# Gated linear attention into an MLP mixer: batch 2 of the channel mixer's input transposed by TensorE in place of the DMA crossbar, with a new order of all instructions

## Chip, cores and metric

One core of one Trainium2 chip. The metric is device time in microseconds; lower is better. Kernel before: 169.14 us, median of 3 runs (169.07 to 169.2).

Short names: PE is TensorE (matmuls; its weight loads are PEld), DVE VectorE, ACT ScalarE, POOL GpSimd, SP SyncE. SP and ACT issue all DMAs, on a queue each.

## What is computed

From q, k, v and alpha, all of shape (4 batches, 8 heads, 768 steps, 48), a recurrence over time, and then a token and channel mixer on its result:

```python
for t in range(S):
    state = alpha[:, :, t, :, None] * state + einsum('bhd,bhe->bhde', k[:, :, t], v[:, :, t])
    y[:, :, t] = einsum('bhd,bhde->bhe', q[:, :, t], state)
x = y.transpose(0, 2, 1, 3).reshape(B, S, H * D)          # (4, 768, 384)
h = maximum(x.transpose(0, 2, 1) @ w_tok1, 0) @ w_tok2     # 768 -> 256 -> 768
u = x + h.transpose(0, 2, 1)
out = u + maximum(u @ w_ch1, 0) @ w_ch2                    # 384 -> 1536 -> 384
```

Inputs, weights and output are float32 in HBM; the matmuls take bf16.

## The kernel before

**Attention** is cut into 12 pieces n = 0 to 11, three of 256 steps for each of the four batches. A piece loads alpha, k, q and v (ld_at, ld_kt, ld_qt, ld_vt; 384 KB each), takes logarithms (ln, for pieces from 3 on P, ln1, lnP, r1), sums them by matmul (cum, cumw for pieces 0 to 2), takes exponentials (E, IE, Et), scales q and k with them (q0r, k0a, qq, kk), casts v to bf16 (vb, and vs0, vs1 for swapped halves), and transposes scaled q and k: pieces 0 to 5 on PE (trq, trk) with a copy out (evq, evk), pieces 6 to 11 by DMA (dq, dk, pq). Then come two half blocks of 128 steps: scores (G0, G1), their mask on DVE (mask0, mask1), key-value sums (K), states (s, sa, sm), outputs (ia, ib for the state's part, y0, y1 for the block's own), and x0, x1, which copy the result to bf16. A number behind the name is the piece: y1_2 is the second half block of piece 2.

**The mixer** runs batch by batch. t1_b_m_i multiplies the six x of a batch with w_tok1, ht is its relu, t2_b_i multiplies with w_tok2, and u_b_i adds x. For the channel mixer u has to be transposed. For batches in `UP` (lines 101 and 300 to 308) PE does it: up_b_p, three groups of six 128x128 transposes into PSUM (`utr`, line 798, matmul at line 803), and ut_b_p, three copies to SBUF on DVE or ACT (`utev`, line 805). For the others SP issues two DMA transposes, ux_b_0 and ux_b_1, one for three u each (`uxbar`, line 667). c1_b_mc_half is the product with w_ch1 (three matmuls of 384 columns, line 811): 12 blocks mc by two halves of the steps; with `UP` a c1 of half 0 waits for ut_0 and ut_1 and one of half 1 for all three, without it for its own ux. rt is its relu on DVE or ACT, c2_b_i_q the product with w_ch2 (line 816), four parts for each of six row blocks i, o adds u, and st stores 192 KB.

**Weights** are loaded in pieces of 384 KB into the same 19 buffers as q, k, v and alpha (`in`) and cast to bf16 by POOL, ACT or DVE: cw_wt10, wt11 (w_tok1), wt20, wt21 (w_tok2), wc10 to wc15 (w_ch1; the first three for mc 0 to 5, the others for mc 6 to 11), wc20 to wc25 (w_ch2; c2's part q needs the pieces that hold its three mc). A load into a used buffer waits until the last reader of the earlier content is done, and its queue waits with it.

**The order** is written out. `ORDER` (line 363) names every operation once, in program order, with a letter for the engine (t PE, s ACT, v DVE, g POOL, y SP); each engine works through its own in that order. `BUFS` (line 432) gives the buffer of every value. Both are the outcome of a search with a planner's costs (lines 35 to 62); the search itself is not in the kernel. [...] And f1_ and f3_ operations are fills: one or three matmuls of 512 columns on zeros (`fill`, line 595), put ahead of PE's operations of pieces 0 to 2 into a PSUM bank that is free; they compute nothing that is used.

```python
UP = (0, 1)                                        # line 101
...
        if b in UP:                                # line 300
            for p in range(3):
                bank = V("one")
...
        else:
            for half in range(2):
                uts.append(P.op(f"ux_{b}_{half}", {"SP": (1240.0, 1240.0)}, ...
```

Of the kernel before, what the change touches and what calls it, by code (L numbers as in the profile page):

```python
# [100 lines left out]
UP = (0, 1)  # L101
# [14 lines left out]
def build(g):  # L116
# [154 lines left out]
    def mixer(b):  # L271
# [27 lines left out]
        uts = []  # L299
        if b in UP:  # L300
            for p in range(3):
# [62 lines left out]
ld_at1s ld_at0y ld_kt0s ld_qt0y ld_qt1s ld_vt0y f1_cumw1t f1_cumw0t f3_cumw0t f3_cumw1t ld_kt1y f3_G00t ln0s ln1s  # L364
cumw0t ld_at2y cumw1t E0s f1_trq0t IE0s qq0v f1_G00t Et0s ld_vt1y IE1s kk0v f1_trk1t trq0t E1s f1_trk0t trk0t Et1s
vb0s f1_trq1t f1_K0t ld_vt3y evk0v qq1g evq0s K0t f3_trk1t s0_0v ld_qt2y ld_at3s sa1_0v vs0_0g vs1_0s f1_G10t kk1v
ld_kt3y ld_kt2s G1_0t G0_0t ln2s trq1t mask0_0v vb1g trk1t evq1s f3_K1t ldw_wt10y sm1_0g mask1_0v K1t evk1s f1_cumw2t
cumw2t sa0_1v vb3g f3_y1t sm0_1v E2s f1_G01t vs0_1g sa1_1v ia1t G0_1t ln13s P3v f1_trq2t Et2s ld_vt2y IE2s f1_y1t
mask0_1v sm1_1g ld_at4y lnP3s f1_y0t vs1_1v cum3t qq2v y0_0t E3s f3_trq2t r13s x0_0v ib0t ldw_wt20y IE3s y1_0t trq2t
k0a3v ld_qt3y x1_0s ib1t kk2v ldw_wt11y y0_1t f3_G11t kk3v cw_wt10s vs1_3s x0_1s f1_G11t G1_1t f1_K2t evq2s mask1_1v  # L370
f1_trk2t vb2g trk2t vs0_3g K2t ldw_wt21y evk2v y1_1t ldw_wc14y trk3t vs1_2g sa0_2v x1_1s ldw_wc13y kb3s f1_G12t
t1_0_1_0t P4v ldw_wc12y t1_0_1_1t G1_2t ka3v lnP4s sm0_2v f1_G02t ia2t kc3s mask1_2v G0_2t vs0_2g evk3s f3_y2t
cw_wt20g q0r3g f1_y2t mask0_2v ld_at5s t1_0_0_0t t1_0_0_1t ldw_wc15s ib2t t1_0_1_2t cw_wt11s cum4t y1_2t y0_2t qq3g
K3t x1_2v x0_2s t1_0_0_2t t1_0_1_3t s0_3v ld_kt4s t1_0_0_3t t1_0_1_4t cw_wt21s t1_0_1_5t t1_0_0_4t sa1_3v t1_0_0_5t
cw_wc14g ht_0_1s ht_0_0v trq3t E4s t2_0_0t ldw_wc11s t2_0_3t cw_wc13g IE4s u_0_0v t2_0_1t evq3s u_0_3v t2_0_5t ld_qt4y
t2_0_2t u_0_1v t2_0_4t ldw_wc10y u_0_2v up_0_0t cw_wc12s ld_qt5y u_0_5v G0_3t ld_kt5y G1_3t P5g ut_0_0s u_0_4v up_0_1t
up_0_2t ut_0_1v lnP5s cw_wc15g ib3t mask0_3v ut_0_2s cum5t c1_0_9_0t ln14s c1_0_11_1t mask1_3v ldw_wc20s c1_0_8_1t
rt_0_11_1s sm1_3g k0a4g c1_0_8_0t r14s rt_0_9_0v ldw_wc21y c1_0_7_0t rt_0_8_1s rt_0_8_0v cw_wc11s c1_0_10_1t y0_3t
y1_3t rt_0_7_0v kk4v c1_0_6_1t ld_at6s IE5s c1_0_9_1t E5s rt_0_6_1v cw_wc10g ld_vt4y rt_0_10_1s c1_0_11_0t rt_0_9_1v
ldw_wc22y x1_3v trk4t q0r4v c1_0_2_1t c1_0_1_0t evk4s rt_0_11_0v qq4g c1_0_3_0t x0_3s c1_0_4_0t rt_0_1_0s ld_vt6y  # L380
rt_0_3_0v ln15s c1_0_3_1t ldw_wc23y k0a5v ldw_wc24s rt_0_2_1s c1_0_4_1t c1_0_0_0t r15s kk5v cw_wc20s trq4t rt_0_3_1s
rt_0_0_0v cw_wc21g evq4s ka4g q0r5g c1_0_5_1t c1_0_5_0t rt_0_4_1v c1_0_0_1t trk5t rt_0_5_0s ldw_wc25y ld_vt5y
rt_0_5_1v rt_0_4_0v c1_0_10_0t qq5g ld_at7s c1_0_7_1t rt_0_0_1v vb4s G0_4t rt_0_7_1v c1_0_2_0t mask0_4v c1_0_6_0t
cw_wc22g ld_kt6y rt_0_2_0s c1_0_1_1t ln16s evk5v ld_at9y c2_0_0_0t vs0_4s vb6g kb4s ia4t rt_0_10_0v y0_4t kc4s trq5t
x0_4v rt_0_6_0s c2_0_1_0t c2_0_1_1t c2_0_2_0t P6v rt_0_1_1s evq5v vs1_4s cw_wc23g vs0_6s K4t ld_kt7s cw_wc24g
c2_0_4_0t lnP6s sa0_4v c2_0_4_1t cw_wc25s ld_qt6y sm0_4v c2_0_2_1t ld_qt8y r16s sa1_4v c2_0_1_2t vs1_6s cum6t sm1_4g
ld_qt7s G1_4t E6s mask1_4v c2_0_2_2t vb5s c2_0_4_2t IE6s vs1_5g c2_0_2_3t t1_1_1_0t kc5s P7g c2_0_1_3t vs0_5s o_0_2v
ld_at8s c2_0_4_3t o_0_1v k0a6g ln17s K5t t1_1_1_1t lnP7s c2_0_0_1t sa0_5v ld_at10s c2_0_0_2t kk6g o_0_4v r17s G0_5t
st_0_1s G1_5t mask0_5v c2_0_5_0t c2_0_5_1t ib4t P9g dk6y mask1_5v y1_4t t1_1_1_2t ia5t x1_4s t1_1_0_0t y0_5t st_0_4y
c2_0_5_2t x0_5s sm0_5v lnP9s t1_1_1_3t q0r6v t1_1_0_1t t1_1_1_4t ib5t ld_vt7s q0r7v y1_5t t1_1_0_2t c2_0_0_3t qq6v  # L390
x1_5s ln18s t1_1_0_3t cum7t k0a7v t1_1_1_5t t1_1_0_4t IE7s t1_1_0_5t c2_0_5_3t ht_1_1s ht_1_0v dq6y ka6s c2_0_3_0t P8v
E7s t2_1_0t t2_1_2t o_0_0v r18s kb6g kk7g u_1_0v u_1_2v t2_1_3t st_0_2s ld_qt9y c2_0_3_1t t2_1_1t t2_1_4t ld_vt8s
u_1_3v ld_kt8s t2_1_5t kc6s u_1_1v ln110s c2_0_3_2t up_1_1t q0r8g u_1_5v st_0_0y dk7y u_1_4v up_1_0t ut_1_0s K6t cum9t
vb7g ut_1_1v o_0_5v IE9s vs0_7v P10g c2_0_3_3t E9s s0_6v up_1_2t ln19s pq6s ut_1_2v c1_1_6_0t c1_1_9_0t kb7g qq7g
c1_1_10_1t o_0_3v sa1_6v ld_at11s c1_1_8_1t rt_1_10_1v r19s c1_1_6_1t rt_1_6_0v ld_kt11s c1_1_7_0t lnP8s rt_1_8_1v
sm1_6g dq7y c1_1_10_0t ka7s rt_1_6_1v c1_1_11_0t c1_1_5_1t rt_1_10_0s vs1_7v rt_1_7_0v rt_1_9_0s r110s cum8t rt_1_5_1v
c1_1_4_0t IE8s vb8v c1_1_1_1t rt_1_4_0s ld_kt9s rt_1_11_0v c1_1_9_1t c1_1_0_0t q0r9v rt_1_1_1s c1_1_3_1t c1_1_2_0t
vs1_8v E8s rt_1_0_0s qq8v rt_1_9_1s c1_1_5_0t c1_1_8_0t kc7s rt_1_3_1s dq8y P11g rt_1_2_0v rt_1_8_0s K7t ld_kt10s
c1_1_11_1t c1_1_7_1t rt_1_5_0s sa0_7v ld_vt9y c1_1_4_1t ld_qt10s sm0_7v rt_1_7_1s sa1_7v k0a8g c1_1_2_1t rt_1_11_1s
st_0_3y rt_1_4_1v c1_1_0_1t rt_1_2_1s c1_1_1_0t sm1_7v rt_1_0_1s kk8v G0_6t rt_1_1_0s G1_6t lnP11s c2_1_4_0t ib6t  # L400
mask1_6v vs0_8s dk8y lnP10s c2_1_3_0t mask0_6v k0a9g pq7g st_0_5y c1_1_3_0t c2_1_3_1t c2_1_4_1t c2_1_3_2t rt_1_3_0s
pq8s qq9v y0_6t y1_6t x0_6s kk9v c2_1_3_3t c2_1_4_2t x1_6s G0_7t o_1_3v G1_7t dk9y vb9v cum10t mask1_7v t1_2_0_0t
c2_1_4_3t E10s kb9g c2_1_0_0t ln111s vs0_9s ka9g dq9y o_1_4v c2_1_0_1t IE10s vs1_9g mask0_7v k0a10g st_1_4s ld_vt10y
c2_1_0_2t kc8s ib7t c2_1_1_0t q0r10v kc9s G1_8t r111s mask1_8v kk10g c2_1_0_3t c2_1_1_1t t1_2_0_1t o_1_0v y1_7t K8t
x1_7s G0_8t sa0_8v dk10y st_1_3s c2_1_1_2t mask0_8v sm0_8g c2_1_1_3t ia7t y0_7t qq10g pq9s o_1_1v ia8t t1_2_1_0t
cum11t x0_7v K9t y0_8t t1_2_1_1t s0_9v E11s ib8t y1_8t t1_2_1_2t IE11s t1_2_0_2t k0a11g sa1_9v t1_2_0_3t dq10y x0_8s
t1_2_1_3t x1_8v G0_9t G1_9t mask0_9v t1_2_1_4t ld_vt11y t1_2_1_5t t1_2_0_4t t1_2_0_5t ht_2_1s st_1_1y c2_1_2_0t ka10g
ht_2_0s mask1_9v kk11g c2_1_2_1t kb10s t2_2_3t vb10s t2_2_5t u_2_3v t2_2_4t ib9t u_2_5v y1_9t kc10g sm1_9g t2_2_1t
u_2_4v x1_9s pq10g t2_2_0t c2_1_2_2t ux_2_1y u_2_0v y0_9t u_2_1v t2_2_2t vs0_10g x0_9s c2_1_2_3t G0_10t c2_1_5_0t
ia10t vs1_10s ld_qt11s mask0_10v c2_1_5_1t c2_1_5_2t u_2_2v K10t o_1_2v y0_10t ux_2_0y c2_1_5_3t sa0_10v x0_10s  # L410
c1_2_4_1t o_1_5v sm0_10g c1_2_11_1t st_1_5y dk11y rt_2_4_1s c1_2_8_1t rt_2_11_1s q0r11g sa1_10v c1_2_9_1t st_1_2y
c1_2_2_1t rt_2_9_1v qq11g c1_2_5_1t rt_2_2_1v c1_2_0_1t c1_2_7_1t rt_2_0_1v rt_2_5_1v c1_2_4_0t vb11g rt_2_7_1s dq11y
c1_2_0_0t c1_2_1_0t sm1_10v rt_2_0_0s c1_2_1_1t vs0_11v rt_2_8_1v st_1_0y kc11s rt_2_4_0s rt_2_1_1v c1_2_10_0t
c1_2_10_1t rt_2_1_0v c1_2_3_1t rt_2_10_1v pq11g c1_2_3_0t rt_2_3_1v c1_2_7_0t rt_2_3_0v K11t c1_2_6_1t rt_2_10_0v
sa0_11v c1_2_9_0t rt_2_6_1s c1_2_2_0t sm0_11g rt_2_9_0v vs1_11s rt_2_7_0s G1_11t G1_10t mask1_11v G0_11t c2_2_4_0t
c2_2_4_1t mask0_11v c2_2_4_2t c2_2_4_3t ib11t y1_11t mask1_10v x1_11s c1_2_5_0t ib10t t1_3_1_0t t1_3_1_1t t1_3_0_0t
rt_2_5_0v o_2_4v t1_3_0_1t y1_10t st_2_4y x1_10v ia11t t1_3_0_2t y0_11t t1_3_1_2t c1_2_11_0t x0_11v rt_2_2_0v
t1_3_1_3t t1_3_0_3t t1_3_1_4t t1_3_1_5t c2_2_5_0t c1_2_8_0t rt_2_8_0s ht_3_1s rt_2_11_0s c1_2_6_0t t1_3_0_4t t1_3_0_5t
c2_2_5_1t c2_2_0_0t rt_2_6_0s c2_2_5_2t ht_3_0s c2_2_5_3t t2_3_4t o_2_5v t2_3_1t t2_3_3t u_3_4v st_2_5y c2_2_1_0t
t2_3_5t t2_3_0t u_3_3v c2_2_0_1t u_3_5v c2_2_0_2t c2_2_0_3t o_2_0v u_3_0v u_3_1v c2_2_1_1t t2_3_2t u_3_2v ux_3_1y  # L420
c2_2_3_0t ux_3_0y c2_2_3_1t c2_2_2_0t c2_2_3_2t st_2_0y c2_2_2_1t c2_2_1_2t c2_2_2_2t c1_3_3_1t c2_2_2_3t c1_3_8_1t
# [453 lines left out]
```

## Time and profile before

| what | value |
|---|---|
| median of the runs | 169.14 us (169.07 to 169.2) |
| the profiled execution: time, span | 169.17 us, 167.4 us |
| mean granted clock of PE | 0.990 |
| PE busy | 159.3 us, 1752 matmuls |
| of it fills (line 593, zs) | 15.6 us, 47 matmuls |
| of it the transposes of u (line 803) | 2.8 us, 36 matmuls |
| DVE, ACT, POOL busy | 123.9, 93.2, 67.4 us |
| DMA read, written | 25.17 MB, 4.72 MB |
| first t2_0, first c1_0, last matmul's end | 35.50, 39.94, 164.45 us |
| from issue to landing, median: q load on SP, DMA transpose of u | 6.8, 3.2 us |

The span runs from the first to the last instruction; the time also holds what lies around them. All instants are counted from the span's start. The chain of waits starts at the last instruction and goes back, at each step to what released it. Matmuls overlap in the pipeline, so the duration of one is longer than the step from one to the next.

### The profile page before, as it was taken

What the parts mean: (1) busy time and instruction counts of PE and PEld (TensorE: products, weight loads), DVE (VectorE), ACT (ScalarE), POOL (GpSimd) and SP (SyncE); (2) the same over time, 40 slices, a digit from 0 to 9 for tenths busy, and PEclk for the clock granted to TensorE, in tenths of its full rate; (3) what the DMA queues carried; (4) which work ended last, traced back from release to release, by engine and by line L of the source; (5) the groups of instructions that cost most, each with busy time, mean ns of one, the idle gap of its engine ahead of it and who ended that gap; (6) DMA issues with size and microseconds to landing.
All of it is one profiled execution on the core that took longest, in us unless ns stands there. A gap on an engine that the chain in (4) does not pass through costs nothing.

```text
span 167.4 us, 4360 instructions
## 1 busy us (share of the span) xinstructions
PE 159.3 (95%) x1752; PEld 100.6 (60%) x1752; DVE 123.9 (74%) x220; ACT 93.2 (56%) x173; POOL 67.4 (40%) x80
## 2 busy tenths in 40 slices
PE   7888689999999999999999999999999999999992
PEld 2445366656666766675666667665576655665562
DVE  4168696989979968999999999787995453555333
ACT  3796557797796993858989647632321301411200
POOL 4035314695159658089045579836400000000000
PEclk9999969999999999999999999999999999999999
DMA  4999999898999999999989986789201135110132
GB/s 125 325 324 323 338 294 306 292 309 245 342 359 359 296 323 300 243 253 236 304 175 278 176 244 112 178 190 197 79 0 51 47 70 146 69 47 0 47 141 94
DMA packets 74531, 34.48 MB, mean 206 GB/s; under 512 B 67984, under 2 KB 73488, under 8 KB 74512
## 3 DMA queue, kind: packets, MB, share of 16 engines
q1 hardware_dynamic: 49504, 22.32, 52.5%
q10 hardware_dynamic: 25008, 11.90, 24.9%
q8 instruction: 13, 0.21, 0.5%
q14 instruction: 6, 0.05, 0.1%
HBM read 25.17 MB, written 4.72 MB: 178 GB/s over the span
## 4 chain that ended last, share of the span: by engine, by line
PE 78%; DMA 10%; POOL 3%; DVE 3%; ACT 2%; issue 1%; SPq 0%; POOLq 0%
PE ps L816 28%; PE ps L811 28%; PE ps L593 10%; PE ps L792 5%; DMA in<-in_v_dram 5%; PE ps L787 4%; DMA in<-in_moe_w_ch_dram 2%; DMA in<-in_alpha_dram 2%; PE ps L654 1%; PE ps L803 1%; POOL vb L685 1%; POOL pkq L642 1%; ACT E L626 1%; ACT IE L626 1%; DVE gtm L700 1%
## 5 line engine op out<-in xcount | busy, mean ns | idle before, releaser
L816 PE MATMUL ps<-wc,rt 128*128 128x384 bf16 (+1 forms) x300 | 53.7, 320 | 0.0
L811 PE MATMUL ps<-ut,wc 128*128 128x384 bf16 x288 | 50.9, 326 | 0.0
L782 ACT ACTIVATE rt<-ps 128x384 bf16<-128x384 f32 x44 | 21.0, 493 | 36.2 <-PE ps L811 35.8
L811 PEld LDWEIGHTS <-wc 128*128 128x128 bf16 x288 | 27.5, 98 | 17.4 <-issue 0.2
L816 PEld LDWEIGHTS <-rt 128*128 128x128 bf16 x300 | 27.8, 98 | 16.4
L700 DVE TENSOR_TENSOR gtm<-ps,mk 128x1024 bf16<-128x1024 f32 x24 | 28.6, 1219 | 4.2 <-PE ps L593 4.1
L784 DVE TENSOR_SCALAR rt<-ps 128x384 bf16<-128x384 f32 x52 | 26.5, 552 | 5.9 <-PE ps L811 5.7
L820 DVE TENSOR_TENSOR o<-ps,u 128x384 f32<-128x384 f32 (+1 forms) x25 | 13.4, 538 | 16.6 <-PE ps L816 16.4
L593 PE MATMUL ps<-zs 128*128 128x512 bf16 x47 | 15.6, 442 | 1.6 <-DVE zs L496 1.1
L642 POOL TENSOR_TENSOR pkq<-in,E 128x768 bf16<-128x768 f32 x7 | 12.7, 1814 | 9.7 <-DVE tpk L685 8.3
L684 ACT CAST x<-ps 128x384 bf16<-128x384 f32 x16 | 7.6, 480 | 12.0 <-PE ps L593 10.8
L685 POOL CAST vb<-in 64x384 bf16<-64x384 f32 (+1 forms) x14 | 9.0, 642 | 12.2 <-PE ps L593 5.5
L796 DVE TENSOR_TENSOR u<-ps,x 128x384 bf16<-128x384 f32 x24 | 12.0, 550 | 1.2 <-PE ps L792 0.9
L787 PE MATMUL ps<-x,wt 128*128 128x384 bf16 x48 | 11.5, 325 | 0.0
L753 POOL TENSOR_TENSOR ss<-tmp,E 128x384 bf16<-128x384 f32 x9 | 7.5, 836 | 7.3 <-DVE tmp L750 5.0
L750 DVE TENSOR_TENSOR tmp<-ps,ss 128x384 f32<-128x384 f32 x16 | 8.8, 553 | 1.2 <-POOL ss L753 0.3
L792 PE MATMUL ps<-ht,wt 128*128 128x384 bf16 x48 | 9.3, 326 | 0.0
L684 ACT CAST vb<-in 64x384 bf16<-64x384 f32 (+1 forms) x15 | 9.0, 599 | 0.3
L593 PE MATMUL ps<-tpq,tpk 48*64 48x128 bf16 x384 | 8.7, 220 | 0.1
L593 PEld LDWEIGHTS <-tpk 48*64 48x64 bf16 x384 | 6.0, 106 | 4.5 <-issue 3.8
L593 PE MATMUL ps<-vb,gtm 128*128 128x48 bf16 x192 | 8.5, 186 | 0.1
L685 POOL CAST wc<-in 128x768 bf16<-128x768 f32 x8 | 6.5, 826 | 5.0 <-DVE pkk L642 4.4
(91 smaller groups left out, 218.4 us busy)
## 6 DMA issues: line engine op xcount, KB each, us to landing
in<-in_v_dram SPq DMA_DIRECT2D x10, 384.0 KB, 6.2
in<-in_alpha_dram ACTq DMA_DIRECT2D x8, 384.0 KB, 5.9
in<-in_q_dram SPq DMA_DIRECT2D x8, 384.0 KB, 6.8
in<-in_k_dram ACTq DMA_DIRECT2D x8, 384.0 KB, 6.1
in<-in_moe_w_ch_dram SPq DMA_DIRECT2D x8, 384.0 KB, 6.8
out_dram<-o SPq DMA_DIRECT2D x15, 192.0 KB, 2.3
in<-in_alpha_dram SPq DMA_DIRECT2D x4, 384.0 KB, 6.5
in<-in_q_dram ACTq DMA_DIRECT2D x4, 384.0 KB, 6.2
```

Source lines behind the costliest of these rows:

```text
L593: return self.pe.matmul(out, lhsT=lhsT, rhs=rhs, start=start, stop=stop, skip_group_check=True)
L642: self.shared(self.eng[e].tensor_tensor(self.t(dst)[:, :, :, 0:D], self.t(src).rearrange("p h s d -> p s h d"), bass.AP(tensor=f.tensor, o ...
L684: return self.act.copy(d, s)
L685: return self.shared(self.eng[e].tensor_copy(d, s))
L700: self.nc.vector.tensor_tensor(self.t(gtm)[:, hf, :, :], self.pair(gp).rearrange("p a (j t) -> p (a j) t", t=128), bass.AP(tensor=m.tensor ...
L782: self.act.activation(d, s, AF.Relu)
L784: self.nc.vector.tensor_scalar_max(d, s, 0.0)
L787: self.pe.matmul(self.bank(bank)[:, 0:HD], lhsT=self.wt1[:, kc, m * 128 : m * 128 + 128], rhs=self.t(x), start=(kc == 0), stop=(kc == NS - 1))
L792: self.pe.matmul(self.bank(bank)[:, 0:HD], lhsT=self.wt2[:, kc, i * 128 : i * 128 + 128], rhs=self.t(hts[kc]), start=(kc == 0), stop=(kc = ...
L811: self.pe.matmul(self.bank(bank)[:, 0:HD], lhsT=self.wc1[:, kc, mc * 128 : mc * 128 + 128], rhs=self.t(ut)[:, 3 * half : 3 * half + 3, kc, ...
L816: self.pe.matmul(self.bank(bank)[:, 0 : cz - ca], lhsT=self.t(rts[mc][0])[:, i * 128 : i * 128 + 128], rhs=self.wc2[:, mc, ca:cz], start=( ...
L820: self.nc.vector.tensor_tensor(self.t(o)[:, ca:cz], self.bank(bank)[:, 0 : cz - ca], self.t(u)[:, i % 3, ca:cz], ALU.add)
```

## The change

`UP` gets batch 2, so that its u is transposed on PE (up_2_0 to up_2_2, ut_2_0 to ut_2_2) and ux_2_0 and ux_2_1 are gone; batch 3 keeps the DMA. `ORDER` and `BUFS` are new throughout: of the operations that both have, 171 are on another engine than before (49 of the 96 rt among them: 32 from DVE to ACT, 17 the other way), and the number of fill matmuls goes from 47 to 51.

```diff
-UP = (0, 1)
+UP = (0, 1, 2)
...
-ld_at1s ld_at0y ld_kt0s ld_qt0y ld_qt1s ld_vt0y f1_cumw1t f1_cumw0t f3_cumw0t f3_cumw1t ld_kt1y f3_G00t ln0s ln1s
...
+ld_at1s ld_at0y ld_kt0s ld_qt0y ld_qt1s ld_vt0y f1_trq1t ld_kt1y f1_cumw0t f1_cumw1t f1_trq0t f3_cumw1t f3_cumw0t
...
```

The part of `ORDER` ahead of the first c1_0, sorted by engine. Before:

```
PE: f1_cumw1 f1_cumw0 f3_cumw0 f3_cumw1 f3_G00 cumw0 cumw1 f1_trq0 f1_G00 f1_trk1 trq0 f1_trk0 trk0 f1_trq1 f1_K0 K0 f3_trk1 f1_G10 G1_0 G0_0 trq1
  trk1 f3_K1 K1 f1_cumw2 cumw2 f3_y1 f1_G01 ia1 G0_1 f1_trq2 f1_y1 f1_y0 cum3 y0_0 f3_trq2 ib0 y1_0 trq2 ib1 y0_1 f3_G11 f1_G11 G1_1 f1_K2 f1_trk2
  trk2 K2 y1_1 trk3 f1_G12 t1_0_1_0 t1_0_1_1 G1_2 f1_G02 ia2 G0_2 f3_y2 f1_y2 t1_0_0_0 t1_0_0_1 ib2 t1_0_1_2 cum4 y1_2 y0_2 K3 t1_0_0_2 t1_0_1_3
  t1_0_0_3 t1_0_1_4 t1_0_1_5 t1_0_0_4 t1_0_0_5 trq3 t2_0_0 t2_0_3 t2_0_1 t2_0_5 t2_0_2 t2_0_4 up_0_0 G0_3 G1_3 up_0_1 up_0_2 ib3 cum5
ACT: ld_at1 ld_kt0 ld_qt1 ln0 ln1 E0 IE0 Et0 IE1 E1 Et1 vb0 evq0 ld_at3 vs1_0 ld_kt2 ln2 evq1 evk1 E2 ln13 Et2 IE2 lnP3 E3 r13 IE3 x1_0 cw_wt10 vs1_3
  x0_1 evq2 x1_1 kb3 lnP4 kc3 evk3 ld_at5 ldw_wc15 cw_wt11 x0_2 ld_kt4 cw_wt21 ht_0_1 E4 ldw_wc11 IE4 evq3 cw_wc12 ut_0_0 lnP5 ut_0_2
DVE: qq0 kk0 evk0 s0_0 sa1_0 kk1 mask0_0 mask1_0 sa0_1 sm0_1 sa1_1 P3 mask0_1 vs1_1 qq2 x0_0 k0a3 kk2 kk3 mask1_1 evk2 sa0_2 P4 ka3 sm0_2 mask1_2
  mask0_2 x1_2 s0_3 sa1_3 ht_0_0 u_0_0 u_0_3 u_0_1 u_0_2 u_0_5 u_0_4 ut_0_1 mask0_3
POOL: qq1 vs0_0 vb1 sm1_0 vb3 vs0_1 sm1_1 vb2 vs0_3 vs1_2 vs0_2 cw_wt20 q0r3 qq3 cw_wc14 cw_wc13 P5 cw_wc15
SP: ld_at0 ld_qt0 ld_vt0 ld_kt1 ld_at2 ld_vt1 ld_vt3 ld_qt2 ld_kt3 ldw_wt10 ld_vt2 ld_at4 ldw_wt20 ld_qt3 ldw_wt11 ldw_wt21 ldw_wc14 ldw_wc13 ldw_wc12
  ld_qt4 ldw_wc10 ld_qt5 ld_kt5
```

After:

```
PE: f1_trq1 f1_cumw0 f1_cumw1 f1_trq0 f3_cumw1 f3_cumw0 f1_trk0 f1_trk1 cumw0 f3_trk1 cumw1 trq0 f1_K0 trk0 K0 f1_G00 f3_G00 f1_K1 G0_0 trq1 f3_K1
  f1_G10 G1_0 K1 trk1 f1_cumw2 cumw2 f1_G01 f3_y0 G0_1 f1_y0 ib0 f1_trq2 f1_y1 f3_y1 f1_trk2 ib1 y0_0 y1_0 f3_trq2 cum3 trq2 f3_G11 f1_G11 G1_1 ia1
  trk2 f3_y2 y0_1 y1_1 f1_G12 f1_K2 K2 G1_2 t1_0_0_0 trk3 t1_0_0_1 f1_y2 f1_G02 G0_2 t1_0_0_2 t1_0_1_0 ia2 t1_0_1_1 ib2 t1_0_0_3 t1_0_1_2 y0_2
  t1_0_1_3 y1_2 K3 t1_0_1_4 t1_0_0_4 t1_0_1_5 t1_0_0_5 trq3 t2_0_3 t2_0_0 t2_0_1 cum4 t2_0_2 t2_0_4 t2_0_5 up_0_0 up_0_1 ib3 G0_3 G1_3 up_0_2
ACT: ld_at1 ld_kt0 ld_qt1 ln0 ld_vt1 ln1 E0 Et0 IE0 IE1 Et1 E1 vb0 evq0 ld_at3 ld_kt2 vs0_0 ln2 ldw_wt10 evq1 evk1 vs0_3 E2 ln13 IE2 Et2 vs0_1
  ldw_wt11 lnP3 r13 x0_0 IE3 E3 evq2 vb2 evk2 x0_1 vs1_2 kb3 vs0_2 cw_wt11 kc3 lnP4 cw_wt20 x0_2 x1_2 ld_kt4 ht_0_0 evq3 ln15 IE4 E4 ln14 lnP5 ut_0_0
  r15
DVE: qq0 kk0 qq1 evk0 s0_0 kk1 sa1_0 mask0_0 mask1_0 sa0_1 sm0_1 sa1_1 vs1_0 mask0_1 sm1_1 qq2 kk2 x1_0 k0a3 mask1_1 kk3 x1_1 sa0_2 mask1_2 mask0_2
  qq3 evk3 s0_3 ht_0_1 sa1_3 u_0_3 u_0_0 u_0_1 u_0_2 u_0_4 u_0_5 ut_0_1 mask0_3
POOL: vb1 sm1_0 vb3 vs1_3 P3 cw_wt10 vs1_1 ka3 P4 sm0_2 q0r3 cw_wt21 P5 cw_wc13 cw_wc14 cw_wc15 sm1_3
SP: ld_at0 ld_qt0 ld_vt0 ld_kt1 ld_at2 ld_vt3 ld_qt2 ld_kt3 ld_vt2 ld_at4 ld_qt3 ldw_wt20 ldw_wt21 ld_at5 ldw_wc13 ldw_wc14 ldw_wc15 ldw_wc12 ld_vt6
  ldw_wc10 ldw_wc11 ld_qt4 ld_at6
```

Around the transposes of batch 2 the new order of PE reads t2_2_2, c2_1_5_1, y0_9, c2_1_5_2, up_2_1, G0_10, y1_9, up_2_2, up_2_0, ia10, c2_1_5_3, y0_10, K10, and then the first c1_2 (c1_2_0_1); ut_2_1 and ut_2_2 are on ACT, ut_2_0 on DVE. The loads of w_ch2 keep their place: wc25 is the 42nd load, in the old order the 41st.

## The prediction

> **What bounds the kernel now.** I read the page first (busy shares, slices), then the chain of waits, then the groups by line, and last the timeline of each engine, on whose rows I put the names of the order by counting along the engine.
>
> ```profile
> span 167.4 us, 4360 instructions
> ...
> PE 159.3 (95%) x1752; PEld 100.6 (60%) x1752; DVE 123.9 (74%) x220; ACT 93.2 (56%) x173; POOL 67.4 (40%) x80
> ...
> PE   7888689999999999999999999999999999999992
> ...
> PEclk9999969999999999999999999999999999999999
> ```
>
> PE is full from the seventh slice on. Before that it has holes, and its clock falls once. The chain of waits says where the one state ends and the other begins:
>
> ```profile
> 10.19 7.60 DMA in<-in_v_dram
> 17.79 0.05 issue
> 17.84 0.83 POOL vb L685
> ...
> 33.16 1.83 POOL pkq L642
> 34.99 0.05 issue
> 35.04 0.62 PE ps L654 x8
> ...
> 111.01 0.49 PE ps L816 x3
> 111.50 8.31 PE ps L811 x51
> ...
> 164.45 0.02 issue
> 164.48 0.36 DVE o L820
> ```
>
> Up to 35.04 us the chain runs through loads, POOL, DVE and ACT: the load of v of attention piece 3, its cast, and so on to qq3 on POOL (33.16 to 34.99), which trq3 waits for. From 35.04 to 164.45 it is PE alone, with 0.03 us of issue in it. So there are two questions: when does PE's unbroken run begin, and how much work is in it. I mark the beginning by the first matmul of the first c1_0, at 39.94 in the timeline. From there PE works 124.5 us to 164.45, and 2.95 us of evict and store follow inside the span. The profiled execution took 169.17, which is 1.77 over its span and 0.03 over the median 169.14.
>
> **The transposes themselves.** The rows that price them:
>
> ```profile
> L803 PE MATMUL ps<-idn,u 128*128 128x128 bf16 x36 | 2.8, 219 | 0.0
> ...
> L684 ACT COPY ut<-ps 128x768 bf16<-128x768 bf16 x3 | 2.4, 800 | 1.2 <-PE ps L803 0.9 <-DVE u L796 0.2
> ...
> L685 DVE COPY ut<-ps 128x768 bf16<-128x768 bf16 x3 | 1.7, 551 | 0.1
> ```
>
> Added on PE: three groups of six. In the chain twelve took 0.67 us at 73.50 and six 0.34, so 18 cost 0.057 x 18 = 1.03 us, on a PE that has nothing else to hide them: the full 1.03 goes on the end. Added beside it: two copies on ACT (0.80 each) and one on DVE (0.55). Their cover is the PE work that stands between the last up_2 and the first c1_2 in the new order: ia10 0.17, one c2 0.49, y0_10 0.20 and K10 0.34, together 1.2 us against at most 0.8; without it PE would stop for some 0.8. Removed: two DMA transposes, 2 issues on SP of 1.24 us. They gain nothing on PE now: ux_2_1 landed at 111.32 and the c1_2 that needs it began at 111.36 with no idle time before it; stores behind them on SP are on nobody's path.
>
> [...]
>
> **The order.** It is all new, and its largest effect is ahead of 40 us. I walk the new order there; durations are steps from start to start on a busy engine in the timeline of before. DVE: mask 1.14 to 1.2, 768-wide product 0.87, 384-wide work 0.47 to 0.55. ACT: wide exp 0.70, evq 1.25, evk 0.95, cast 0.75, narrow work 0.45 to 0.5. PE: a fill 0.22, a transpose group 0.45, G 0.35. Loads land one per 1.21 us (384 KB at 325 GB/s) in order of issue: the 9th landed at 14.02, the 18th at 25.86.
>
> Step 1. at2 is now the 9th load, so ln2 on ACT starts at 14.05 and ends at 14.9. Behind it ACT issues wt10. This is an operation whose cost before does not show: ACT's third open load.
>
> ```profile
> 2.09 1.78 ACTq L534 DMA_DIRECT2D in<-in_q_dram  x1
> ...
> 10.03 0.45 ACTq L534 DMA_DIRECT2D in<-in_alpha_dram  x1
> ```
>
> With two loads open an issue took 1.78 us, with none 0.45, and SP's fourth took 2.36; what stands behind it on ACT (evq1) waits so long. Below nothing it cannot be. I take 1.0, since at3 will be half in by then; ends 0.4 and 2.36. evq1 then runs 15.8 to 17.05, evk1 to 18.0.
>
> Step 2. v of piece 3 is the 10th load, not the 11th, and no longer waits behind v1 in SP's queue: it lands near 15.2 instead of 17.79, and vb3, sm0_1 and P3 leave the path. Late next is evk1: G0_1 waits for it and for one group of three fills, so mask0_1 ends at 20.3 (before 21.62).
>
> Step 3. DVE then runs without a hole: sm1_1, qq2, kk2, x1_0, k0a3 end at 23.4 (before, kk2 alone at 24.80). PE reaches G1_1 at 23.85, mask1_1 ends at 25.15 (before 28.26), kk3 at 26.0, sa0_2 at 27.05 (K2 is the last to come), mask1_2 at 28.2, mask0_2 at 29.4 (before 32.93).
>
> Step 4. qq3 is on DVE: 0.9 us, ending at 30.3, where POOL took 1.82 and ended at 34.98. Late next is ACT: after evk2 (25.95) stand ten pieces, x0_1 to x1_2, 5.35 us, so x1_2 ends at 31.3. Two t1, the ht, and t2_0 begins at 32.4 (before 35.50).
>
> Step 5. From t2_0 on: six u of 0.47 from 32.9 end at 35.75, then ut_0_0 on ACT, 0.7: 36.5. The weights do not hold it: wc15 is the 25th load (the 25th of before landed at 35.13), and its cast takes 0.8. I say 36.7 for the first c1_0, so 3.24 us earlier.
>
> Four more fills (0.9 us) lie in PE's holes: useful PE work from cumw0 to t2_0 is 14.4 us and fills 8.6, of 26.5 us. Without the holes they would cost 0.9; step 3 counts those on the path.
>
> Against this: 1.03 for the transposes, and 0.29 for cum5, the one useful piece that the old order had done ahead of c1_0 and the new has not. Then a loss between 36.7 and 60, since all is needed earlier and loads are not faster. c1_0_5_1 comes 5.5 us after the first c1_0, at 42.2, and needs wc10 and wc11, the 29th and 30th load. At the pace of 1.21 from the 25th on, the 30th lands at 41.2, its cast (0.85) ends at 42.05: no loss. In the rows of before the 30th landed at 43.00: 43.85, a loss of 1.6. wc25, the 42nd, is needed 21.1 us after the first c1_0, at 57.8; by pace its cast ends at 56.5, by the row of before (57.79) at 58.6. In before wc10 stood behind qt4, which had to wait for a buffer until 36.55, and in the new order it does not; so nearer to the pace, but not at it: 0.8. DVE is no reason for more, its work falls from 119 to 111 us (sums by the steps above), ACT's rises from 93 to 103 of 168.
>
> Sum: 169.17 - 3.24 + 1.03 + 0.29 + 0.8 = 168.05, say **168.1**, 0.6% under the median.
>
> **The rivals.**
> *Weights late.* The loads run no earlier than before, and the whole 1.6 to 2.0 us is lost at c1_0_5_1 and the c2_0 behind it. For it: DMA moves 290 to 360 GB/s in nearly every slice to 50 us. Against it: the free buffers above. 168.9 to 169.3, **169.1**, no difference. Chance 0.15.
> *No loss at all.* Every load fits: **167.2**, and 166.7 if wt10's issue costs 0.4. Chance 0.13.
> *ACT holds the start.* This one is slower. The new order puts 8 of the first 18 loads on ACT's queue, where the old had 5, and 24.1 us of ACT work ahead of t2_0 instead of 21.0. If each of the three further issues (vt1, wt10, wt11) blocks ACT for the 1.8 to 2.4 us of the rows above, some 3 us of it land on steps 1 and 4, t2_0 begins at 35.5 as before, and only the added work is left: 169.17 + 1.32 = **170.5**. It decides from a first c1_0 later than 37.8 on. For it: ACT has only some 2.4 us of slack in 26.5. Against: instructions already handed to ACT run on during an issue (at 10.03 a cast ran beside it). Chance 0.24.
> *The transposes do not overlap.* If each took its own row's 219 ns, 18 cost 3.94, 2.9 more than I count: **171.0**. [...] The twelve in 0.67 us speak against it. Chance 0.03.
> That the change does not do what it says is excluded: the new order has 44 more PE rows, 18 transposes and 4 fills with their weight loads, and two DMA transposes fewer.
>
> **How the numbers follow.** My forecast has 0.45, its own range 167.2 to 168.9. What a measurement here can tell from no change is about 0.2%, 168.8 to 169.5. Faster: 0.43 of the forecast and the 0.13, 0.56. Same: most of late weights and the forecast's end, 0.16. Slower: ACT, the transposes and a little of late weights, 0.28. The range 166.8 to 170.6 leaves out the upper part of ACT's rival, the transposes and the lowest start, about 0.14.
>
> **What would show it.** Right: first L792 matmul near 32.4 and first L811 near 36.7; the pkq product of piece 3 on DVE, done near 30.3; 54 transposes at the same 0.057 pace; PE idle after 36.7 of about 0.8 us, ended by a cast of wc. Wrong: ACT issues of over 1.5 us in 5 to 20 us with ACT idle behind them, or a second fall of the clock behind 40 us.

## The result and the profile after

The kernel after took 169.6 us (169.09 to 170.12, 20 runs), the kernel before 169.05 (167.53 to 169.29, 20 runs, on the same chips): 1.0052 times as long by all runs, 95% interval 1.0032 to 1.0072. (By the two medians alone it is 1.0033; before's runs fall into two groups, of which more below.) The change makes it slower by half a per cent; 168.1 was forecast. Runs that a disturbance lengthened (two of b_nogap's 12, one each of b_gap5's and b_gap8's) are left out of every comparison here.

The page of after: span, engines, slices of PE, its clock. Then, of the groups by line with their shapes kept apart, the transposes of u: times, busy us, mean ns of one, idle time ahead.

```profile
span 167.8 us, 4423 instructions
...
PE 159.6 (95%) x1774; PEld 100.7 (60%) x1774; DVE 115.1 (69%) x202; ACT 100.7 (60%) x189; POOL 70.8 (42%) x85
...
PE   7979899899999999999999999999999999999982
...
PEclk9999999999999999999999999999999999999999
```

```profile
L803 PE MATMUL ps<-idn,u 128*128 128x128 bf16 x54 | 4.0, 219 | 0.0
```

The start is what the prediction said. PE is full earlier, its clock does not fall, the first of the six t2_0 begins at 32.76 us (35.50 before; 32.4 was forecast), and the first c1_0 at 36.84 (39.94 before; 36.7 was forecast). Yet the last matmul ends at 164.85, later than the 164.45 of before. The last but one slice of PE's row (159.4 to 163.6 us) shows where: 8, where before has a 9. The chain of waits names it (start, duration, what):

```profile
138.91 3.74 DMA out_dram<-o
...
143.22 0.56 DVE o L820
...
143.82 6.01 PE ps L811 x36
...
159.22 3.92 DMA out_dram<-o
...
163.27 0.37 DVE o L820
...
163.68 1.17 PE ps L816 x12
```

In before the chain from 35 us on was PE alone. Here it twice runs from a store of a finished output tile (DMA) through o on DVE to PE. There are three buffers for o: a new o waits until the store out of its buffer has landed, the PSUM bank that o is to empty stays full, and the product that needs this bank waits on PE. In before, where the stores of the end land in 1.9 us, PE never waits for one. In the DMA issues of the page (tile, queue, count, KB, median us to landing) the stores on SP's queue took, first before and then after:

```profile
out_dram<-o SPq DMA_DIRECT2D x15, 192.0 KB, 2.3
```

```profile
out_dram<-o SPq DMA_DIRECT2D x15, 192.0 KB, 3.8
```

These are medians of 15 stores of the whole run, most of which nobody waits for. The four stores ahead of the two stops, st_2_2 (issued at 138.91), st_3_3 (158.74), st_3_4 (159.22) and st_3_2 (160.69), took 3.74, 3.94, 3.92 and 2.93 us. In before the same four took 1.84, 1.95, 1.88 and 1.87.

**The balance.** I compared the steps from one PE operation to the next with the pace that the operation has on a busy PE. What goes beyond the pace is a stop.

| term, us | forecast | measured |
|---|---|---|
| first c1_0 earlier | -3.24 | -3.10 |
| 18 transposes of batch 2 | +1.03 | +1.03 |
| cum5 now behind the first c1_0 | +0.29 | +0.29 |
| further stops of PE, 37 to 140 us | +0.80 | +0.91 (2.94 against 2.03) |
| stops of PE behind 140 us (0.43 at 143.8, 0.84 at 163.7) | none | +1.27 |
| last matmul's end against 164.45 | -1.12 | +0.40 |

So one term was missing, 1.27 us. A second thing only the runs show: **the kernel before has two kinds of runs**. Of 140 runs of it beside the experiments below, 84 show a mean granted clock of 0.99 and a median of 169.10 us, 56 a clock of 1.00 and 167.68. (So a median of before depends on how many runs of each kind are in it.) The profile of the prediction is of the first kind. After's runs all have 1.00. The questions are then why the stores came late, what the second kind of before means for the 3.1 us at the start, and what the named part of the change, the transposes, costs by itself.

### The profile page after: what moved, and what is told of

Read it like the earlier page. It is cut to its first block, busy times and chain, and to the rows that moved or that the text cites. A ratio compares the mean times of both kernels' runs of the same rounds, so it can differ in the third digit from the quotient of the medians.

```text
span 167.8 us, 4423 instructions
## 1 busy us (share of the span) xinstructions
PE 159.6 (95%) x1774; PEld 100.7 (60%) x1774; DVE 115.1 (69%) x202; ACT 100.7 (60%) x189; POOL 70.8 (42%) x85
## 4 chain that ended last, share of the span: by engine, by line
PE 41%; POOL 9%; issue 7%; DMA 5%; DVE 4%; ACT 1%; SPq 0%; ACTq 0%; POOLq 0%; DVEq 0%
PE ps L816 17%; PE ps L811 15%; PE ps L593 5%; DMA out_dram<-o 5%; PE ps L787 2%; POOL pkq L642 2%; POOL in L578 2%; POOL pkk L642 2%; PE ps L792 1%; DVE o L820 1%; POOL in L638 1%; DVE rt L784 1%; POOL kt L685 1%; POOL vb L685 1%; DVE ss L753 1%
## 5 line engine op out<-in xcount | busy, mean ns | idle before, releaser
L816 PE MATMUL ps<-wc,rt 128*128 128x384 bf16 (+1 forms) x300 | 55.5, 320 | 0.8 <-DVE o L820 0.7
L782 ACT ACTIVATE rt<-ps 128x384 bf16<-128x384 f32 x59 | 27.0, 490 | 29.8 <-PE ps L811 29.5
L784 DVE TENSOR_SCALAR rt<-ps 128x384 bf16<-128x384 f32 x37 | 19.4, 553 | 14.0 <-PE ps L811 13.8
L642 POOL TENSOR_TENSOR pkk<-in,IE 128x768 bf16<-128x768 f32 x7 | 12.7, 1819 | 5.2 <-ACT rt L782 4.0
L685 POOL CAST vb<-in 64x384 bf16<-64x384 f32 (+1 forms) x13 | 7.5, 575 | 16.0 <-DVE pkk L642 11.2
L684 ACT CAST vb<-in 64x384 bf16<-64x384 f32 (+1 forms) x17 | 10.8, 643 | 2.9 <-DMA in<-in_k_dram 0.9
L642 DVE TENSOR_TENSOR pkq<-in,E 128x768 bf16<-128x768 f32 x7 | 6.7, 957 | 6.0 <-ACT E L626 4.6
L578 POOL TENSOR_TENSOR in<-in 128x384 f32<-128x384 f32 x8 | 8.0, 1000 | 5.8 <-issue 3.0
L642 POOL TENSOR_TENSOR pkq<-in,E 128x768 bf16<-128x768 f32 x5 | 9.1, 1824 | 3.0 <-DVE vb L685 1.9
L634 POOL TENSOR_TENSOR in<-in,in 128x384 f32<-128x384 f32 x7 | 7.0, 1001 | 4.2 <-DMA in<-in_k_dram 2.6
```

The costliest lines, as they stand in the source:

```text
L642: self.shared(self.eng[e].tensor_tensor(self.t(dst)[:, :, :, 0:D], self.t(src).rearrange("p h s d -> p s h d"), bass.AP(tensor=f.tensor, o ...
L684: return self.act.copy(d, s)
L782: self.act.activation(d, s, AF.Relu)
L784: self.nc.vector.tensor_scalar_max(d, s, 0.0)
L816: self.pe.matmul(self.bank(bank)[:, 0 : cz - ca], lhsT=self.t(rts[mc][0])[:, i * 128 : i * 128 + 128], rhs=self.wc2[:, mc, ca:cz], start=( ...
```

## Experiments: why the stores are late

*Theory.* In the trace each kernel has packets of 16 KB on DMA queue q8, "instruction" (packets, MB, share), first before and then after:

```profile
q8 instruction: 13, 0.21, 0.5%
```

```profile
q8 instruction: 14, 0.23, 0.6%
```

With 1752 + 1752 PE instructions (matmuls and weight loads) in before and 1774 + 1774 in after, that is one packet for some 250 to 270 of them. In after the last two start at 140.16 and 159.91 us and take 1.23 and 1.43 us, right among the late stores. In before the last is at 145.60, behind five of the six stores of batch 2 and over before the sixth is issued at 147.04, and none comes later. The 44 more PE rows of the change (18 transposes, 4 fills, each with its weight load) moved them. The trace does not say whose code a packet holds. That it is PE's, and a packet of it a code fetch, I read from this count; whether the packets go where PE's instructions put them, and whether they cost time, is what the runs put to the test.

*Rival.* The new order puts stores on both DMA queues at once and next to the DMA transposes of batch 3, and they would be late without any fetch.

**Output tiles with buffers of their own** (a_obuf). The 13 o of batches 2 and 3 lie in buffers of loads that are over by then:

```diff
     def t(self, v):
+        if v.cls == "o" and v.buf > 2:
+            return self.T["in"][...].rearrange("p h s d -> p (h s d)")[:, 0:HD]
```

> The new kernel, but each o of batches 2 and 3 has a buffer of its own (in memory of the loads' buffers, unused by then), where three were shared; nothing else changes. Code fetch theory (a 16 KB packet of PE's code holds one DMA engine for some 2 us, stores that are under way land late, and with three o buffers the next o, its PSUM bank and PE wait): the two PE stops at 143.8 and 163.7 go, some 1.2 us, time near 168.3 to 168.6; stores still land late where a fetch meets them. Rival, the two queues hinder each other's stores: same gain here. Rival, PE stops for another reason than the stores: no change, 169.6.

Measured: 168.5 us (167.44 to 168.85), 1.1 under after; against before 1.0016 (0.9982 to 1.005). (After itself was not run again beside the experiments; the two kinds of before have medians of 167.60 to 167.84 and 169.06 to 169.17 us on every chip used.) The fetches still start at 140.44 and 160.23, st_2_2 and st_3_4 still take 3.76 and 3.45 us, and PE has no stop behind 140 us. From the first c1_0 to the last matmul PE takes 126.67 us, after 127.99; of these 1.32 us the total shows 1.1, since the first c1_0 of this profile is 0.32 later. So the late stores cost what they cost through the three buffers. The two packets take 1.20 and 1.01 us, less than the 2 us of my theory.

**Fetches moved, buffers as they were** (a_shift). Of the fills, 21 matmuls of 512 columns become four of 128 each: the same work, 126 more PE instructions.

```diff
     def fill(self, bank, count, split=False):
...
+            if split:
+                for c in range(4):
+                    self.mm(self.bank(bank)[:, 128 * c : 128 * c + 128], self.zs, z, True, True)
+                continue
```

> The new kernel, with 21 of the 512-column fills of the start cut into four of 128 columns each: 63 matmuls and 63 weight loads more, same columns, same PE time; later instructions of PE sit 126 further back in its code. Code fetch theory: the fetches of 140.2 and 159.9 come some 10 us earlier, near 130 and 150, where no store matters; stores of the end land in 1.9 us again, the PE stops go, 168.3 to 168.6. Rival, two queues hinder each other: stores at 138.9 and 158.7 still take 3.7 to 3.9 us, 169.6.

Measured: 168.69 us (168.21 to 168.89), 0.9 under after. From the first c1_0 to the last matmul PE takes 126.68 us, 1.31 less than in after; the first c1_0 is 0.44 later. The last fetches start at 130.73 and 151.51. The order of all operations, their queues and buffers are those of after. The stretch from 156 to 167 us, by DMA queue (packets, MB, share) and issues (count, KB, median us to landing), of after:

```profile
q10 hardware_dynamic: 576, 0.59, 15.4%
q1 hardware_dynamic: 357, 0.47, 11.7%
q8 instruction: 1, 0.02, 0.8%
...
out_dram<-o ACTq DMA_DIRECT2D x2, 192.0 KB, 3.4
out_dram<-o SPq DMA_DIRECT2D x2, 192.0 KB, 2.9
```

and of a_shift:

```profile
q10 hardware_dynamic: 576, 0.59, 15.1%
q1 hardware_dynamic: 348, 0.46, 11.3%
...
out_dram<-o ACTq DMA_DIRECT2D x2, 192.0 KB, 1.9
out_dram<-o SPq DMA_DIRECT2D x2, 192.0 KB, 1.9
```

One packet of 16 KB more or less, and the same stores take 3.4 or 1.9 us. On PE (start, duration, line; in brackets the idle time ahead and what ended it) after has

```profile
157.30 5.70 PE L816 MATMUL ps<-wc,rt 128*128 128x384 bf16 x40
163.68 1.15 PE L816 MATMUL ps<-wc,rt 128*128 128x192 bf16 x12 [0.68 <-DVE o L820]
```

and a_shift one piece:

```profile
157.27 6.69 PE L821 MATMUL ps<-wc,rt 128*128 128x384 bf16 x52
```

The rival falls: queues and neighbours are the same, the lateness is gone. st_2_2 takes 2.27 us. st_2_0 and st_2_5, near the DMA transposes of batch 3, are late in both (3.07 and 3.50 us here), and nobody waits for them.

**The same done to before** (b_shift): 11 fills cut, 66 more instructions.

> The kernel before, with 11 fills cut into four in the same way: 66 instructions more in PE's code. Code fetch theory: a fetch that the kernel before had at 145.6 comes at about 140.5, and one more at about 160.3, among the last stores: these land 1.5 to 2 us late, and the time rises by 0.5 to 1.2 us, to about 170. Rival, two queues: nothing changes, 169.1.

Measured: at clock 1.00 168.66 us (7 runs) against 167.68 of before, at 0.99 169.66 (5 runs) against 169.09; all runs 1.006 (1.0023 to 1.0097). Fetches at 139.56 and 160.56; stores of 1.90 and 1.95 us now take 2.66 and 2.79, a DMA transpose of batch 3 issued at 137.69 takes 4.82 instead of 3.22, and PE stops for 0.38 us behind it. Before, with nothing but its code moved, gets slower by 0.6 to 1.0 us. In the profiled execution PE takes 0.79 us more from the first c1_0 to the last matmul; the rest of it is mainly a stop at 74.5 us, behind a copy on ACT, whose cause was not traced.

**Both remedies in one** (a_both).

> The kernel after, with a buffer for each output tile of batches 2 and 3 and with 21 fill matmuls cut into four narrow ones, both edits of the last runs in one. Theory: each alone took away the same two stops of PE at the end (1.27 us), so together they give no more than either: 168.5 us, between 168.3 and 168.7. Rival, they act on two different things (buffers on PE's stops, fetches on the stores at the very end): 167.8 or less.

Measured: 168.7 us (168.23 to 168.84), as either alone, and no stop behind 140 us. So they act on one and the same thing. It also says that 168.5 to 168.7 is what the new order gives without the accident, and that is still 0.8 to 1.0 over the runs of before at clock 1.00.

## Experiments: the two kinds of runs of before

**The stop in PE filled, other fills left out** (b_nogap). In before PE stands from 19.77 to 21.68 us; five fills more there (f1_y0 of six matmuls), and five others (f1_trk2, f1_K2, f3_y2) left out, so that the number of instructions stays.

> The kernel before, with five more fill matmuls in f1_y0 (where PE stood still for 1.9 us from 19.8 and its clock was halved for 3.4 us), and f1_trk2, f1_K2 and f3_y2 left out, so that the number of instructions stays. Theory of the clock: the runs of before at 167.5 to 168.1 are those without the fall of the clock, and the others those with it; this one has clock 1.00 throughout and takes 167.6 in every run. Rival, the fall costs nothing, since PE waits for others until 35 us anyway: 169.1 as before, with the same spread.

Measured: 168.0 us (167.55 to 168.47, 10 runs), all at clock 1.00. That is 0.3 over before's runs at 1.00 on the same chip (167.68), where I expected 167.6; its profile, of one of the runs left out, does not say why.

**Before once more** (b_look).

> The kernel before, unchanged, for one more profile. Its runs fall in two groups: 13 of 35 with a mean granted clock of 0.99 took 168.9 to 169.4 us (the profile shown is one of these), 22 with a clock of 1.00 took 167.4 to 168.6. Theory: the whole difference arises at the clock's fall at 21.85 us, so a profile of the second group shows no fall, the first c1_0 near 38.5 us instead of 39.94, and 124.5 us from there to the last matmul as before; then the new order's start at 36.84 is worth 1.7 us and not 3.1. Rival: the groups differ somewhere behind 40 us, and the first c1_0 is at 39.9 in both.

Measured: 168.78 us at 0.99, the same kind again: first c1_0 at 39.60. No profile of before itself at 1.00 was caught; one of the other kind came with b_up2 (below), which has before's order up to batch 2, with some fills cut into narrower ones: first c1_0 at **38.52**. The stretches of both (length, busy us and instructions of PE, PEld, DVE, ACT and POOL, granted clock, DMA share, GB/s), first before:

```profile
18.00:20.00 2.00, 1.62 (x24) 0.65 (x22) 1.17 (x3) 1.34 (x4) 1.17 (x2) 1.00 1.16 340
20.00:22.00 2.00, 0.32 (x6) 0.26 (x7) 1.97 (x3) 0.52 (x1) 0.83 (x1) 0.96 1.16 345
22.00:24.00 2.00, 2.00 (x23) 1.17 (x21) 1.97 (x5) 1.30 (x3) 0.00 (x0) 0.50 0.96 248
24.00:26.00 2.00, 2.00 (x33) 1.76 (x31) 1.67 (x2) 1.52 (x3) 0.21 (x1) 0.68 1.03 314
```

and b_up2:

```profile
20.00:22.00 2.00, 0.32 (x7) 0.26 (x8) 1.97 (x3) 0.52 (x1) 0.83 (x1) 1.00 1.11 325
22.00:24.00 2.00, 2.00 (x57) 2.00 (x54) 1.97 (x5) 1.83 (x5) 0.00 (x0) 1.00 1.05 269
24.00:26.00 2.00, 2.00 (x52) 1.80 (x48) 2.00 (x3) 1.98 (x4) 0.20 (x1) 1.00 1.05 312
```

PE is idle alike between 20 and 22 us (0.32 busy of 2.00). Behind it the clock falls to 0.50 in the one execution and not in the other, and that puts the first c1_0 1.42 us later.

**The stop filled, nothing left out** (b_gap5, b_gap8): f1_y0 with 6 and with 9 matmuls.

```diff
-                     emit=lambda e, z=z: g.fill(bank, z)) for z in (1, 3)]
+                     emit=lambda e, z=z: g.fill(bank, 9 if (z, nm) == (1, "y0") else z)) for z in (1, 3)]
```

> The kernel before, with five more fill matmuls (1.1 us) in the stop of PE from 19.77 to 21.68 us and nothing left out elsewhere. Theory: the two groups of the kernel before differ by the clock's fall behind this stop and by nothing else, 1.4 us. With the stop cut to some 0.8 us no run shows a mean clock of 0.99, the first c1_0 lies near 38.5, and the median is 167.7 (167.4 to 168.5), which is under both kernels. The ten more PE instructions bring the code fetch from about 144.2 to 143.4, behind the stores of batch 2, and no new one ahead of the end. Rival: the fall has another cause and comes as often as in the kernel before, median 168.9; or the first c1_0 stays at 39.6 or later without a fall.

> As b_gap5 with eight more fills (1.8 us), which fill the stop but for some 0.15 us. Theory: the same 167.7, or up to 0.2 more where the last fill delays cum3, and again no run at 0.99. The sixteen more PE instructions bring a further code fetch near the last matmuls, at about 162.9 to 163.1 in a run at clock 1.00, if PE gets that far; if it does, the last stores land up to 1 us late and the median is 168.2 to 168.7, which would be the code fetch again and not the clock.

Measured: b_gap5 168.17 us (167.68 to 169.27, 11 runs), 0.9982 of before (0.9947 to 1.0018); b_gap8 **168.05** (167.55 to 168.40, 11 runs), 0.9957 (0.9926 to 0.9987), against 169.12 for before on the same chip. None of these runs shows 0.99. The page of b_gap8:

```profile
span 165.8 us, 4371 instructions
...
PE 159.8 (96%) x1760; PEld 100.5 (61%) x1760; DVE 123.8 (75%) x220; ACT 93.1 (56%) x173; POOL 67.4 (41%) x80
...
PE   7988999999999999999999999999999999999992
...
PEclk9999999999999999999999999999999999999999
```

Its first c1_0 is at 38.37, 0.15 ahead of b_up2's: in this execution, the fastest of its 11, the fills cost nothing in the stop. From the first c1_0 to the last matmul PE takes 124.5 us in before, b_look and b_gap8 alike. So as far as these profiles show, the clock's fall is the difference of the two kinds (1.42 us at the first c1_0, 1.42 between their medians), and b_gap8 is under the medians of both kernels. It is not under before's runs at 1.00: five of these on its chip have a median of 167.60, 0.45 less, and no trace shows what the 0.45 are.

Two misses. Four runs of b_gap5 took 169.2 at clock 1.00. Two of them have spans of 166.2 and 166.3 us, where the median of its runs is 166.2: their whole excess lies outside the span, 3.0 us instead of 1.7, before the first or behind the last instruction. The third has a span of 166.9 and 2.3 us outside it, the fourth a span of 167.4; no trace explains these. And the further fetch that I expected of b_gap8 near 163 came at 161.21 and made no store late in the profiled execution: the next one was issued 0.08 us after it had ended. Whether it does so in the slower runs is not shown.

## Experiments: the transposes by themselves

**Before's order, batch 2 on PE by hand** (b_up2), with 26 fills cut so that the fetches lie at 128.5 and 149.1 us, away from the stores:

```diff
-UP = (0, 1)
+UP = (0, 1, 2)
...
-c2_1_5_0t ia10t vs1_10s ld_qt11s mask0_10v c2_1_5_1t c2_1_5_2t u_2_2v K10t o_1_2v y0_10t ux_2_0y c2_1_5_3t
+c2_1_5_0t up_2_2t ia10t vs1_10s ut_2_2s ld_qt11s u_2_2v mask0_10v c2_1_5_1t up_2_0t ut_2_0s c2_1_5_2t up_2_1t
+ut_2_1s K10t o_1_2v y0_10t c2_1_5_3t
```

> The kernel before with its own order, and in it batch 2 of u transposed on PE by hand (up_2 and ut_2 in the place of the two DMA transposes); 26 fill matmuls are cut into four narrow ones, so that PE's code fetches fall near 131 and 151 us, away from the stores of the end. The part of the change that its words name, alone. By my theory the transposes cost their PE time, 1.03 us, and nothing else: 168.7 us in runs at clock 1.00 and 170.1 at 0.99, against 167.7 and 169.1 of the kernel before. Rival one, the DMA transposes held something up that PE transposes set free: no difference, or faster. Rival two, the transposes do not overlap in this place: 3.9 us more.

Measured: at clock 1.00 168.65 us against 167.84 on the same chip, at 0.99 170.05 against 169.06; all runs 1.0039 (1.0006 to 1.0072). So 0.8 to 1.0 us for 1.03 of work: the change that the title names costs what its matmuls take, and gives nothing back. At 219 ns each, the duration of one in its row, the 18 would have cost 3.94 us, nearly four times as much. That row does not say how far several overlap; the step from one to the next is 57 ns (twelve in 0.67 us), and the runs decide for the 57.

**The same without the cut fills** (b_up2_raw).

> As b_up2 (the order of before, batch 2 of u transposed on PE by hand), but with no fill cut: 36 more PE instructions than before and nothing that keeps the code fetches away. Theory: 36 instructions bring PE's last two code fetches to about 142.4 and 162.2 us in a run at clock 1.00 (before has one at 145.6 and none behind it), and the second meets the last stores, issued at 163.4 to 164.4, whose landing is the end of the kernel: 0.5 to 1.0 us slower than b_up2, so 169.2 to 169.7 at clock 1.00 and 1.4 more at 0.99, with no new stop of PE behind 145 us. Rival, the fetches cost nothing in themselves and the new order's stores were late for another reason: the same as b_up2, 168.7 and 170.05.

Measured: at clock 1.00 169.16 us (168.60 to 169.61, 8 runs), at 0.99 170.46 (4 runs): 0.4 to 0.5 over b_up2, at the lower end of what I expected, and with a spread of 1.0 us where b_up2 has 0.6. (It ran on another chip; over before's runs there it is 1.5 and 1.3, where b_up2 is 0.8 and 1.0.) In the profiled execution (169.84 us at 0.99, the fastest of the four) the fetches lie at 143.47 and 163.50, where theory put them; the first makes a store take 3.32 us, the second ends as the next store is issued, and nothing waits. So in this execution the one fetch met a store and the other just missed one. That the excess of the other runs is the fetch is not shown: no trace here has the last stores late.

**The new order, transposes undone** (a_dma2, a_dma2b to a_dma2d): a_both with batch 2 by DMA, u_2_4, u_2_5, u_2_3 first and ux_2_1 behind them. The first try (169.89 us, where I expected 167.5 to 168.0) is read for its time alone: in it ib9 overwrites the bank that mask1_9 reads, and u of batch 2 overwrites u of batch 1 that o_1_2 still needs. In the second (a_dma2b) PE stops for 1.55 us at 107.3, since c2_1_5 uses half of the bank pair of mask1_9:

> The new order with the transposes undone: as a_both (a buffer for each output tile of batches 2 and 3, fills cut), but batch 2 of u transposed by DMA. u_2_4, u_2_5, u_2_3 come first, then the DMA transpose of that half, then the other three; ib9 stands next to y1_9, and y0_10 and K10 behind the first three c1_2. Theory: the 1.03 us of the transposes are gone from PE and at most 0.5 us of waiting for the first DMA transpose comes in their place: 167.6 to 168.2 us against 168.7 of a_both, under the medians of both kernels. Rival: the first DMA transpose lands over a us after PE asks for it, and the kernel is no faster than a_both.

Measured 169.81 us (169.47 to 170.28). In the third c2_1_5 has another bank, but y0_9 waits 1.17 us for the bank of t2_2_0:

> As a_dma2b, with two PSUM banks exchanged: there c2_1_5 used the second bank of G1_9's pair, and waited 1.55 us for mask1_9, which that order puts behind four pieces on DVE; now c2_1_5 has the bank of t2_2_5 and the first c1_2 the other. So this is the new order with the transposes of batch 2 undone and no wait of the edit's own making. Theory: against a_both (168.7) the 1.03 us of the transposes are gone, and the DMA transpose, issued near 105.7 and 3.5 us under way, lands before PE asks for it near 109.4: 167.6 to 168.0 us. Rival: the transposes by PE were not what a_both pays, and the time stays at 168.5 or above.

Measured 169.49 us (168.69 to 169.99). From the first c1_0 to the last matmul PE took 127.46 us, a_both 126.71; the stops between 100 and 120 us are 1.79 more, so the work is 1.03 less, as it must be. In the fourth these waits are gone too:

```diff
-t2_2_1t kk11g pq10s mask1_9v t2_2_0t u_2_1v c2_1_5_0t u_2_0v t2_2_2t
+t2_2_1t kk11g pq10s t2_2_0t u_2_0v mask1_9v c2_1_5_0t u_2_1v t2_2_2t
```

> As a_dma2c, without the waits that the edit itself made there (PE stood 1.17 us ahead of y0_9, whose bank t2_2_0 had, and 0.44 ahead of c1_2_4_1, behind K10): t2_2_0 now has the bank of t2_2_4, u_2_0 stands ahead of mask1_9, c1_2_9_1 is the first c1_2, c1_2_10_0 goes ahead of c1_2_4_0. In the profile of a_dma2c PE's work from the first c1_0 to the last matmul was 1.03 us less than in a_both, and 1.79 us of these waits ate it. Theory: without them 168.7 - 1.03 + 0.1 to 0.4 = 167.8 to 168.1 us, the new order's start without the price of the transposes, under the medians of both kernels. Rival: the DMA transposes cost a wait of their own wherever they stand, since 3.4 to 3.8 us of landing has to be covered, and the time stays at 168.5 or above.

Measured: 168.91 us (168.66 to 169.67), 1.0008 of before (0.9983 to 1.0034), 0.2 over a_both. PE of a_dma2d at batch 2:

```profile
108.51 0.42 PE L613 MATMUL ps<-tpq,tpk 48*64 48x128 bf16 x16 [0.70 <-ACT x L708]
...
110.52 1.64 PE L835 MATMUL ps<-ut,wc 128*128 128x384 bf16 x9 [0.63 <-DMA ut<-u]
```

The DMA transpose, issued at 105.39, landed at 110.47, and the first c1_2 waited 0.63 us for it; G0_10 had waited 0.70 for x0_9 on ACT, which a_both does not do. So only a part of what this order loses against my 167.8 is the landing, and it does not show that DMA transposes must cost what those on PE cost. I had also overlooked where PE's code fetch lies: here one starts at 107.43 and takes 1.10 us, in the middle of this landing of 5.08 us. In a_dma2c the same transpose was issued at 105.36 and landed in 3.40 us, and the fetch came at 108.89, behind it. The long landing may be the fetch once more; no run separates the two. Whether a search could find an order that covers the landing is open.

## Why the prediction was wrong, point by point

- **What bounds the kernel**: right. PE from the first c1_0 on, and the time follows its first moment and its work.
- **Steps 1 to 5, the start**: right in the outcome, with one wait wrong. mask1_1 ended at 25.28 (25.15 forecast), mask0_2 at 29.74 (29.4), x1_2 at 31.64 (31.3), and the first c1_0 came at 36.84 (36.7). wt10's issue on ACT blocked nothing: evq1 ran from 14.92, and evk1 ended at 17.09 (18.0). But vt3 landed at 16.97 (15.2), and step 2 had taken vb3 and sm0_1 off the path. They stayed on it: POOL cast vb3 from 17.03, DVE stood idle for 0.79 us until sm0_1, which the kernel makes wait for that cast (`shared`, line 671), could begin at 17.88, and mask0_1 came behind that, at 19.55, 1.25 us after the end of G0_1, which step 2 has it wait for. That mask0_1 ended at 20.78 (20.3) is in part luck: the wait that held it was another one and ended at nearly the same time. *ACT holds the start*, the rival with the most weight, is refuted: it needed a first c1_0 later than 37.8.
- **The transposes**: right in pace and in price, 1.03 us, shown by the trace and by b_up2.
- **The loss of 0.8 us**: right in size by luck, wrong in place and cause. wc10 and wc11 landed at 37.66 and 38.71, and *weights late* is refuted; from 37 to 60 us after has only 0.1 more stops than before. The rest is spread over 60 to 120 us (0.41 ahead of a c1_1 at 79.3, 0.29 at K7, 0.25 at K10).
- **The sum**: here the prediction failed. It let PE run to the end without a stop because before did, and counted the 44 new PE rows as time only. They are also code: they moved a fetch into the stores of each of the last two batches. The term for stops behind 140 us was nothing, and it measured 1.27 us. a_obuf and a_shift show it: in different ways each takes 1.3 us off PE's time from the first c1_0 to the last matmul, and 1.1 and 0.9 off the total. With this term, and 0.14 and 0.11 for the start and the small stops, the sum is 168.05 + 1.52 = 169.57; the profiled execution took 169.51.
- **Its own time of before**: I took the profiled 169.17 for the kernel. It holds a fall of the clock that 56 of 140 runs do not have. Without it before's first c1_0 is at 38.4 to 38.8 (three profiles: b_up2, b_gap5, b_gap8), after's at 36.8 to 37.4 (eight profiles with its order of the start). So against a run without the fall the new order gains 0.9 to 1.9 us and not 3.1, which is less than the 2.2 of transposes, cum5 and small stops: it would be slower than such a run without the late stores too, as a_both shows. With the late stores gone (168.5 to 168.7 us), the new order is 0.4 to 0.6 us faster than before's runs with the fall and 0.8 to 1.0 slower than those without it. Nearly half of the gain forecast for the start, 1.4 of 3.2, was the fall, which no profile of the new order shows, and filling the stop alone (b_gap8) avoids it too, in 168.05 us.
- **What I said would show it wrong** (ACT's issues, a second fall of the clock) did not occur. The right place was a DMA queue that the page shows in one row and that I had not read.

## What to carry to other kernels

Look at how many executions of the profiled kind there are before an instant of one profile becomes a term of a sum; here the mean granted clock in the page, 0.990, was the mark. Instructions added to PE moved its later code fetches here (126 more in a_shift: the last two from 140.16 and 159.91 us to 130.73 and 151.51): mark the "instruction" packets of the trace, work out where they go, and see which store or transfer stands there with a reader waiting for its buffer. Count the buffers of a tile that is stored for a late landing, and not only for the usual one: three were enough here at 1.9 us and not at 3.9. (a_obuf gave every tile its own; how few more would do was not tried.)

## What the runs showed of the hardware that I had not expected

- A 16 KB packet of PE's code takes 0.9 to 1.8 us and comes once per some 250 to 270 PE instructions. Stores of 192 KB that were under way or just issued mostly took 2.2 to 3.9 us instead of 1.9 (a_obuf, after, b_shift); one that was nearly over was not late (b_gap8: issued at 140.53, 1.86 us, fetch at 142.04). Which resource they share the trace does not show.
- The clock fell to half for 3.4 us behind a stop of PE of 1.64 us (b_look) and of 1.91 (before), but not behind one of 1.97 (b_up2). So the length of the stop alone does not decide it, and of the runs of before 84 show the fall's clock of 0.99 and 56 do not. What decides it no run shows.
